# A spectral transform with a three-way maximum layer on one core: the input arrives as fp32, and GpSimd casts and turns it

## The chip, the cores and the metric

One core of a Trainium2 chip runs the kernel. The metric is the device time of one execution in microseconds. Three runs of the kernel before took 499.56, 500.29 and 500.31; their median, 500.29, is the time before.

## The reference

```python
x: (8, 3072, 256) fp32
X = np.fft.fft(np.fft.fft(x, axis=1), axis=2).real      # real part of the 2-D transform
x2 = X.reshape(24576, 256)
h = np.maximum(np.maximum(x2 @ w1, x2 @ w2), x2 @ w3)    # w1, w2, w3: 256 x 768
out = h @ w_out                                          # w_out: 768 x 256, fp32
```

So each batch of 3072 positions is transformed over its positions, then over its 256 channels, and the result goes through a feed-forward layer whose nonlinearity is a maximum of three products.

## The kernel before

**The transform over positions** has two stages, since 3072 is 24 times 128. A position is 128·a + bb. In the first stage (`fnet`, line 270) a matmul has as its stationary operand a 96 x 128 piece of the input: 96 partitions are 24 values of a for each of four groups g of 64 channels, and the 128 columns are the values of bb, for one of the 64 channels dl of each group. The moving operand is `m24blk`, a block-diagonal 96 x 96 table of the 24-point transform. So 64 matmuls make the first stage of a batch, one for each dl. They come in 13 groups (`DLS`, line 61), twelve of five matmuls and one of four, in an order that starts at the middle channels. Each group fills one of the two PSUM buffers of the pool `ps_f`, and ScalarE evicts it into `ub` as bf16 (line 272).

VectorE then folds channel d with channel 256 - d: sums go to `zE` and differences to `zO` (lines 280 to 297). That is possible because only the real part is wanted. The second stage multiplies zE and zO, as stationary operands with strided columns, with tables of cosines and sines (lines 318 to 326, 50 matmuls of mostly 128 columns, also through `ps_f`), which gives the tiles `tE` and `tO`, 128 x 1536 each, evicted by ScalarE (line 329). Three matmuls of one column (lines 332 to 334) make `t_mid`, the frequency at the middle. GpSimd copies tE and tO reversed to `tEr` and `tOr` (lines 339 and 340).

**The transform over channels** is not computed on the data: it is folded into the weights. `prep_first` (line 220) subtracts w1 from w2 and w3 on VectorE (line 228), multiplies the differences with the table `md` (line 232), and leaves `gE`, `gO` and `gD`. `prep_second` (line 240) makes `gw` and `gwr`, the product of md, w1 and w_out (lines 247 and 255). Both also take their PSUM from `ps_f`, and both run once, during batch 0.

**The layer.** Since max(a, b, c) = a + max(0, b - a, c - a), a block of 512 tokens needs for each of six columns blocks `jc` of the hidden layer only the two differences. A *unit* is one jc of one block; a batch has 18, three blocks of six. Its first half are four matmuls of 512 columns (lines 349 and 350) into two PSUM banks; ScalarE applies the relu to one of them (line 363), VectorE takes the maximum with the other into `hp` (line 364). Its second half are two more matmuls (line 357), which add gD to the same two banks and so turn the frequencies into their mirror images, and again a relu and a maximum, into `hm`. A batch has 108 unit matmuls. There are two pairs of these banks.

The output of a block is made of four pieces of 128 rows, twice 256 columns wide. Each half is eight matmuls of 256 columns (`l2_half`, lines 367, 369 and 372), so that a batch has 192 output matmuls. VectorE copies a piece out (line 392) and SP stores it (line 399) from one of four `ot` buffers, in two DMAs, or four for the last piece of a batch.

**What sets the order.** The units' loop pulls the output matmuls of earlier blocks from a list, eleven after each unit (`l2_some`, line 448), and the program is then ordered by the compiler's scheduler, which works from its own estimate of each instruction's length. Each engine runs its list in the order that comes out. On GpSimd the start of the program has an order fixed by hand (`manual_schedule`, line 133).

**The input.** `load_x0` (line 97) brings in a batch with 16 DMAs on GpSimd's software queue (line 105), which cast fp32 to bf16 on the way; rows of 64 channels stay together, so that a tile `x0` lies as (bb dl), and the stationary columns of the first stage, at `x0r[:, :, d0 + i]`, are 64 elements apart. There are two x0 buffers. Batches 0 and 1 are loaded at the start, with the weights between them on the same queue, and batch b + 2 after the first block of batch b.

Of the kernel before, what the change touches and what calls it, by code (L numbers as in the profile page):

```python
# [34 lines left out]
def kernel(  # L35
# [16 lines left out]
    nc = tc.nc  # L52

    B, S, D = x.shape
    assert (S, D) == (3072, 256)
    DFF = moe_w1.shape[1]
# [11 lines left out]
    ps_o = ctx.enter_context(tc.tile_pool(name="ps_o", bufs=2, space=bass.MemoryType.PSUM))  # L68
    x0_pool = ctx.enter_context(tc.tile_pool(name="x0", bufs=2))
# [14 lines left out]
    v2_bf = consts.tile([128, 2 * DFF], BF16, tag="v2_bf")  # L84
    v3_bf = consts.tile([128, 2 * DFF], BF16, tag="v3_bf")
# [11 lines left out]
    def load_x0(b, between):  # L97
        x0 = x0_pool.tile([96, 128 * 64], BF16, name="x0", tag="x0")
        xr = x[b].rearrange("(a bb) (g dl) -> g a bb dl", bb=128, g=4)
        x0v = x0.rearrange("p (bb dl) -> p bb dl", dl=64)  # L100
        for ch in range(4):
            if ch in between:
                between[ch]()
            for g in range(4):
                nc.gpsimd.dma_start(  # L105
                    out=x0v[g * 24:(g + 1) * 24, ch * 32:(ch + 1) * 32, :],
                    in_=xr[g, :, ch * 32:(ch + 1) * 32, :])
        return x0
# [17 lines left out]
    def between():  # L126

        nc.gpsimd.iota(kidx, [[1, 13], [24, 128]], base=0, channel_multiplier=0,
                       allow_small_or_imprecise_dtypes=True)
        nc.gpsimd.iota(dvec, [[1, 64], [64, 2]], base=0, channel_multiplier=0,  # L130
                       allow_small_or_imprecise_dtypes=True)

    with tc.manual_schedule(engines={mybir.EngineType.Pool}):
        x0_tiles = {0: load_x0(0, {1: between})}


        for jh in range(2):
            for wsrc, wdst in ((moe_w1, w1_bf), (moe_w2, w2_bf), (moe_w3, w3_bf)):
                nc.gpsimd.dma_start(
                    out=wdst.rearrange("p (fc j) -> p fc j", fc=2)[:, :, jh * 384:(jh + 1) * 384],  # L140
                    in_=wsrc.rearrange("(fc p) j -> p fc j", fc=2)[:, :, jh * 384:(jh + 1) * 384])
        nc.gpsimd.dma_start(out=wout_bf.rearrange("p (jc c) -> p jc c", jc=NJC),
                            in_=moe_w_out.rearrange("(jc p) c -> p jc c", jc=NJC))
        x0_tiles[1] = load_x0(1, {})
# [28 lines left out]
    for (dst, shift) in ((cos_t, 768.0), (sin_t, 0.0)):  # L173
        v = gen.tile([128, 13 * 128], FP32, name="v", tag="v", bufs=2)
        q = gen.tile([128, 13 * 128], FP32, name="q", tag="q", bufs=2)
# [14 lines left out]
    for fc in range(2):  # L190
# [10 lines left out]
        vi = gen.tile([128, 256], INT32, name="vi", tag="vi", bufs=2)  # L201
# [4 lines left out]
        _sin_of_index(nc, md[fc], vm, 256, neg_pi)  # L206

# [12 lines left out]
    def prep_first():  # L220

        for jh in range(2):
            cs = slice(jh * 384, (jh + 1) * 384)
            for i, (wv, vv) in enumerate(((w2_bf, v2_bf), (w3_bf, v3_bf))):
                w3d, v3d, w13d = (t.rearrange("p (fc j) -> p fc j", fc=2)[:, :, cs]
                                  for t in (wv, vv, w1_bf))
                tc.keep_in_program_order(
                    nc.vector.tensor_tensor(out=v3d, in0=w3d, in1=w13d, op=ALU.subtract))
# [8 lines left out]
                nc.vector.tensor_scalar(out=gD[i][:, cs], in0=gO[i][:, cs], scalar1=dif,  # L237
                                        scalar2=None, op0=ALU.mult)
# [25 lines left out]
    def fnet(b, x0):  # L264
        x0r = x0.rearrange("p (bb dl) -> p bb dl", dl=64)
        ub = u_pool.tile([128, 64 * 96], BF16, name="ub", tag="ub")
        for (d0, d1) in DLS:
            ps1 = ps_f.tile([128, 512], FP32, name="ps1", tag="ps")
            for i in range(d1 - d0):
                nc.tensor.matmul(ps1[:, i * 96:(i + 1) * 96], x0r[:, :, d0 + i], m24blk,  # L270
                                 start=True, stop=True)
            nc.scalar.copy(out=ub[:, d0 * 96:d1 * 96], in_=ps1[:, 0:(d1 - d0) * 96])  # L272
# [142 lines left out]

    l2_queue = []
# [9 lines left out]
    for b in range(B):  # L426
# [11 lines left out]
        for blk in range(3):  # L438
# [3 lines left out]
            for jc in range(NJC):  # L442
# [5 lines left out]
                l2_some(11)  # L448
            l2_some(1000)
# [5 lines left out]
            if blk == 0 and b + 2 < B:  # L455
                x0_tiles[b + 2] = load_x0(b + 2, {})
# [33 lines left out]
```

## Time and profile before

| What | us |
|---|---|
| the three runs | 499.56, 500.29, 500.31 |
| the profiled execution, its own time | 499.23 |
| its span | 497.1 |
| ScalarE's relu of a 512-column bank, mean | 0.588 |
| VectorE's maximum into hp, mean | 0.690 |
| GpSimd's DMA instructions, 128 of them, mean | 0.863 |
| GpSimd's reversed copies of tE, mean | 1.471 |

The mean granted clock of TensorE in that execution was 0.993.

How to read the views in the prediction: engines are PE (TensorE's matmuls), PEld (its weight loads), DVE (VectorE), ACT (ScalarE), POOL (GpSimd) and SP (which here only issues DMAs). A row of the time line has the start and the length in us, the engine, the line of the kernel, the operation, its output <- its inputs, the tile's shape and how many instructions the row joins; in brackets stands the idle time before it on that engine, and whose end released it. Matmuls are pipelined, and the ends of matmuls are modelled, so that rows overlap; the distance between two starts is the pace. A row of the windows has the window, its length, then busy time and instructions of PE, PEld, DVE, ACT, POOL and SP, then the granted clock, the busy share of the DMA engines and GB/s. A row of the groups has the count, then busy time and the mean in ns, then idle time ahead of the group and what ended it.

### The profile page before, as it was taken

Reading aid. Unit: us, or ns where it says so; the run is one execution under the profiler, and the core shown is the slowest. Engines: PE = TensorE matmul, PEld = TensorE weight load, DVE = VectorE, ACT = ScalarE, POOL = GpSimd, SP = SyncE. Lnnn points to the kernel's source line nnn. Section 1 sums busy time; section 2 is a strip of 40 time slices with the busy share of each in tenths; the row PEclk is TensorE's granted clock in tenths of the full one; section 3 lists DMA queues with packets and bytes.
Section 4 is the critical chain, followed back from the end, with each engine's and each line's share of the span. In section 5 each row is a group of like instructions: output and inputs, shape, how many; then the busy total and the mean of one; then the engine's idle time right before and its main releaser. Section 6 shows DMA issues by size and latency. Waiting matters only on the chain.

```text
span 497.1 us, 9195 instructions
## 1 busy us (share of the span) xinstructions
PE 453.5 (91%) x3408; PEld 315.6 (63%) x3408; DVE 320.4 (64%) x662; ACT 260.9 (52%) x472; POOL 140.6 (28%) x160
## 2 busy tenths in 40 slices
PE   0056999999999999999999999999999999999995
PEld 0055447785568657785669666875669566866664
DVE  8834674657676576657666567657675666667663
ACT  1355652575436653575446644665457644765440
POOL 9979800029000750029000840048000100020000
PEclk9999899999999999999999999999999999999998
DMA  8999992219921692219911793119911022102122
GB/s 48 75 164 99 98 32 86 84 44 108 105 86 66 59 133 99 73 44 109 126 65 65 74 123 102 65 46 120 134 64 65 22 65 84 65 22 65 65 84 86
DMA packets 163436, 40.05 MB, mean 81 GB/s; under 512 B 136512, under 2 KB 163392, under 8 KB 163392
## 3 DMA queue, kind: packets, MB, share of 16 engines
q0 software_dynamic: 135536, 14.30, 70.6%
q1 hardware_dynamic: 27856, 25.18, 16.1%
q8 instruction: 26, 0.43, 0.4%
q14 instruction: 18, 0.15, 0.1%
HBM read 28.31 MB, written 25.17 MB: 108 GB/s over the span
## 4 chain that ended last, share of the span: by engine, by line
PE 78%; DVE 3%; ACT 2%; POOL 2%; DMA 1%; issue 1%; DVEq 0%; ACTq 0%
PE po L372 23%; PE pse L349 12%; PE pse L357 11%; PE pse L350 11%; PE ps L270 8%; PE po L367 4%; PE po L369 4%; POOL x L105 2%; PE ps L318 2%; DMA x<-in_x_dram 1%; PE ps L324 1%; PE ps L326 1%; ACT stmp L363 1%; PE ps L321 1%; DVE zE L280 1%
## 5 line engine op out<-in xcount | busy, mean ns | idle before, releaser
L363 ACT ACTIVATE stmp<-pse 128x512 bf16<-128x512 f32 (+1 forms) x294 | 167.7, 588 | 164.3 <-PE pse L350 128.6
L364 DVE TENSOR_TENSOR hp<-pse,stmp 128x512 bf16<-128x512 f32 x144 | 99.1, 690 | 99.1 <-PE pse L357 39.8
L105 POOL DMA_DIRECT2D x<-in_x_dram x128 | 109.5, 863 | 8.1 <-DMA x<-in_x_dram 3.6
L349 PE MATMUL pse<-tE,gE 128*128 128x512 bf16 x288 | 108.8, 379 | 1.7 <-DVE hm L364 0.7
L350 PE MATMUL pse<-tO,gO 128*128 128x512 bf16 x288 | 109.1, 380 | 0.0
L364 DVE TENSOR_TENSOR hm<-pse,stmp 128x512 bf16<-128x512 f32 x144 | 99.0, 687 | 11.8 <-ACT stmp L363 9.3
L357 PE MATMUL pse<-tO,gD 128*128 128x512 bf16 x288 | 94.8, 380 | 1.1 <-ACT stmp L363 0.6
L339 POOL COPY tEr<-tE 128x1536 bf16<-128x1536 bf16 x8 | 11.8, 1471 | 289.1 <-ACT tE L329 289.1
L372 PE MATMUL po<-wout_bf,hp 128*128 128x256 bf16 x576 | 92.6, 272 | 0.0
L372 PE MATMUL po<-wout_bf,hm 128*128 128x256 bf16 x576 | 89.1, 272 | 0.1
L270 PE MATMUL ps<-m24blk,x 96*128 96x96 bf16 x512 | 57.4, 250 | 28.8 <-DMA w_bf<-in_moe_w_dram 27.5
L270 PEld LDWEIGHTS <-x 96*128 96x128 bf16 x512 | 55.9, 199 | 33.1 <-DMA w_bf<-in_moe_w_dram 27.4
L392 DVE COPY ot<-po 128x512 f32<-128x512 f32 x96 | 65.5, 684 | 14.5 <-PE po L372 13.8
L372 PEld LDWEIGHTS <-hm 128*128 128x128 bf16 x576 | 56.1, 99 | 17.3 <-DVE hm L364 0.4
L372 PEld LDWEIGHTS <-hp 128*128 128x128 bf16 x576 | 56.2, 100 | 14.2
L272 ACT CAST ub<-ps 128x480 bf16<-128x480 f32 (+1 forms) x104 | 55.4, 554 | 15.6 <-PE ps L270 13.3
L357 PEld LDWEIGHTS <-gD 128*128 128x128 bf16 x288 | 28.1, 98 | 29.8 <-issue 1.5
L350 PEld LDWEIGHTS <-gO 128*128 128x128 bf16 x300 | 29.4, 98 | 27.1 <-issue 12.2
L349 PEld LDWEIGHTS <-gE 128*128 128x128 bf16 x300 | 29.5, 99 | 21.1 <-issue 2.6
L280 DVE TENSOR_TENSOR zE<-ub 128x240 bf16<-128x240 bf16 (+2 forms) x80 | 20.2, 311 | 33.9 <-ACT ub L272 33.9
L367 PE MATMUL po<-gw,tE 128*128 128x256 bf16 x96 | 26.2, 272 | 0.0
L369 PE MATMUL po<-gwr,tOr 128*128 128x256 bf16 x96 | 26.2, 272 | 0.0
(99 smaller groups left out, 359.5 us busy)
## 6 DMA issues: line engine op xcount, KB each, us to landing
out_dram<-ot SPq DMA_DIRECT2D x176, 128.0 KB, 1.7
x<-in_x_dram POOLq DMA_DIRECT2D x128, 96.0 KB, 6.7
out_dram<-ot SPq DMA_DIRECT2D x24, 64.0 KB, 6.7
w_bf<-in_moe_w_dram POOLq DMA_DIRECT2D x6, 192.0 KB, 6.2
out_dram<-ot SPq DMA_DIRECT2D x8, 63.0 KB
wout_bf<-in_moe_w_out_dram POOLq DMA_DIRECT2D x1, 384.0 KB, 8.6
out_dram<-ot SPq DMA_DIRECT2D x1, 8.0 KB
```

Of the source, the lines that this page charges most:

```text
L105: nc.gpsimd.dma_start(out=x0v[g * 24:(g + 1) * 24, ch * 32:(ch + 1) * 32, :], in_=xr[g, :, ch * 32:(ch + 1) * 32, :])
L270: nc.tensor.matmul(ps1[:, i * 96:(i + 1) * 96], x0r[:, :, d0 + i], m24blk, start=True, stop=True)
L272: nc.scalar.copy(out=ub[:, d0 * 96:d1 * 96], in_=ps1[:, 0:(d1 - d0) * 96])
L349: nc.tensor.matmul(pse[:, 0:n], gE[i][:, js], te, start=True, stop=False)
L350: nc.tensor.matmul(pse[:, 0:n], gO[i][:, js], to, start=False, stop=True)
L357: nc.tensor.matmul(pse, gD[i][:, js], to, start=False, stop=True, skip_group_check=True)
L363: nc.scalar.activation(out=stmp[:, 0:n], in_=pses[0][:, 0:n], func=AX.Relu)
L364: nc.vector.tensor_tensor(out=dst, in0=src3, in1=stmp[:, 0:n], op=ALU.max)
L367: nc.tensor.matmul(po, te, gw[:, 0:256], start=True, stop=False)
L369: nc.tensor.matmul(po, to, wo, start=False, stop=False)
L372: nc.tensor.matmul(po, hcols(jc), wout_bf[:, jc * 256:(jc + 1) * 256], start=False, stop=(jc == NJC - 1))
L392: nc.vector.tensor_copy(out=ot, in_=po)
```

## The change

- The input comes as fp32, in four chunks of 32 values of bb for each batch (`load_chunk`), each four DMAs into one of four staging buffers `xs`. For batches 0 and 2 to 7 SP's hardware queue does it; batch 1's chunks are still issued on GpSimd.
- `turn_chunk` copies a chunk from xs to x0, casting it to bf16 and changing its layout from (bb dl) to (dl bb). GpSimd does it for all batches but the first; of batch 0 ScalarE takes half of chunks 1 and 2 and a third of chunk 3, VectorE another third of it.
- The first stage's stationary operand is now `x0r[:, d0 + i, :]`, 128 neighbouring elements.
- In batch b, after units 0 and 3 of blocks 0 and 1 (`TURNS`), one chunk of batch b + 2 is loaded on SP and turned on GpSimd.
- At the start the iotas stand ahead of the loads. Of GpSimd's list, three turns of batch 0 come first, then the weights, then the fourth turn, then batch 1's loads, each followed by its turn.
- `prep_first` subtracts in place and makes all four subtractions ahead of the matmuls; gD is made from PSUM instead of from gO. Two bf16 tiles (v2_bf, v3_bf) and second buffers of the tables' working tiles go.
- In batch 0 VectorE evicts five of the thirteen groups of the first stage.

```diff
+    xs_pool = ctx.enter_context(tc.tile_pool(name="xs", bufs=4))
...
-    def load_x0(b, between):
...
+    def load_chunk(b, ch, engine):
+        xs = xs_pool.tile([96, 32 * 64], FP32, name="xs", tag="xs")
+        xr = x[b].rearrange("(a bb) (g dl) -> g a bb dl", bb=128, g=4)
+        for g in range(4):
+            engine.dma_start(
+                out=xs[g * 24:(g + 1) * 24, :].rearrange("p (bb dl) -> p bb dl", dl=64),
+                in_=xr[g, :, ch * 32:(ch + 1) * 32, :])
+        return xs
+
+    def turn_chunk(xs, x0, ch, copies):
+        src = xs.rearrange("p (bb dl) -> p dl bb", dl=64)
+        dst = x0.rearrange("p (dl bb) -> p dl bb", bb=128)[:, :, ch * 32:(ch + 1) * 32]
+        step = 64 // len(copies)
+        for i, copy in enumerate(copies):
+            hi = 64 if i == len(copies) - 1 else (i + 1) * step
+            copy(dst[:, i * step:hi, :], src[:, i * step:hi, :])
...
+    x0_tiles = {0: new_x0(), 1: new_x0()}
+    first = [load_chunk(0, ch, nc.sync) for ch in range(4)]
...
+    with tc.manual_schedule(engines={mybir.EngineType.Pool}):
+        turn_chunk(first[0], x0_tiles[0], 0, [by_pool])
+        turn_chunk(first[1], x0_tiles[0], 1, [by_pool, by_act])
+        turn_chunk(first[2], x0_tiles[0], 2, [by_pool, by_act])
...
+        turn_chunk(first[3], x0_tiles[0], 3, [by_pool, by_dve, by_act])
+        for ch in range(4):
+            xs1 = load_chunk(1, ch, nc.gpsimd)
+            turn_chunk(xs1, x0_tiles[1], ch, [by_pool])
...
-        x0r = x0.rearrange("p (bb dl) -> p bb dl", dl=64)
+        x0r = x0.rearrange("p (dl bb) -> p dl bb", bb=128)
...
-                nc.tensor.matmul(ps1[:, i * 96:(i + 1) * 96], x0r[:, :, d0 + i], m24blk,
+                nc.tensor.matmul(ps1[:, i * 96:(i + 1) * 96], x0r[:, d0 + i, :], m24blk,
                                  start=True, stop=True)
-            nc.scalar.copy(out=ub[:, d0 * 96:d1 * 96], in_=ps1[:, 0:(d1 - d0) * 96])
+            copy = by_dve if b == 0 and d0 in (25, 35, 15, 10, 5) else by_act
+            copy(ub[:, d0 * 96:d1 * 96], ps1[:, 0:(d1 - d0) * 96])
...
+    TURNS = [(0, 0), (0, 3), (1, 0), (1, 3)]
...
+                if (blk, jc) in TURNS and b + 2 < B:
+                    ch = TURNS.index((blk, jc))
+                    if ch == 0:
+                        x0_tiles[b + 2] = new_x0()
+                    turn_chunk(load_chunk(b + 2, ch, nc.sync), x0_tiles[b + 2], ch, [by_pool])
...
-            if blk == 0 and b + 2 < B:
-                x0_tiles[b + 2] = load_x0(b + 2, {})
```

The scheduler orders the program anew. Three places matter for the prediction. Lines after the change are 24 to 27 higher in `fnet` and the layer: 296 is the first stage (270 before), 345 the second (318), 394 to 399 the output (367 to 372), 426 the store (399), 366 the reversed copy (339).

TensorE where batch 0 ends, in the kernel before: x0_149 is batch 1's input, and po_1160 an output piece of batch 0.

```order
L270 LDWEIGHTS x0_149
L270 MATMUL ps1_973<-m24blk_85,x0_149 128x96
L367 LDWEIGHTS tE_369
L367 MATMUL po_1160<-gw_104,tE_369 128x256
L369 LDWEIGHTS tO_370
L369 MATMUL po_1160<-gw_104,tO_370 128x256
L372 LDWEIGHTS hp_783
L372 MATMUL po_1160<-wout_bf_96,hp_783 128x256
...
L270 LDWEIGHTS x0_149
L270 MATMUL ps1_980<-m24blk_85,x0_149 128x96
```

There the output matmuls of batch 0 stand between the groups of batch 1's first stage. The same place after the change, where x0_125 is batch 1's input and po_1320 the last output piece of batch 0:

```order
L394 LDWEIGHTS tEr_458
L394 MATMUL po_1320<-gw_105,tEr_458 128x256
L396 LDWEIGHTS tOr_459
L396 MATMUL po_1320<-gwr_106,tOr_459 128x256
L399 LDWEIGHTS hm_812
L399 MATMUL po_1320<-wout_bf_97,hm_812 128x256
...
L296 LDWEIGHTS x0_125
L296 MATMUL ps1_987<-m24blk_88,x0_125 128x96
```

All 108 unit matmuls and all 192 output matmuls of batch 0 now stand ahead of batch 1's first stage.

GpSimd's list around batches 0 and 1 in the kernel before, where x0_149 and x0_596 are the inputs of batches 1 and 2:

```order
L105 DMA x0_149<-in_x_dram 24x32x64 x16
L339 COPY tEr_438<-tE_369 128x1536
L340 COPY tOr_439<-tO_370 128x1536
L105 DMA x0_596<-in_x_dram 24x32x64 x16
L339 COPY tEr_1145<-tE_1076 128x1536
```

After the change, the end of that stretch, where x0_125 is batch 1's input, x0_513 batch 2's, and xs_514 holds batch 2's first chunk:

```order
L116 CAST x0_125<-xs_251 96x64x32
L101 DMA xs_257<-in_x_dram 24x32x64 x4
L116 CAST x0_513<-xs_514 96x64x32
L116 CAST x0_125<-xs_257 96x64x32
L366 COPY tEr_1173<-tE_1104 128x1536
```

And SP's list after the change, where ot_1351 is the last piece of batch 0 and xs_562 batch 2's second chunk; in the kernel before this list holds stores alone:

```order
L426 DMA out_0_dram<-ot_1316 128x256 x2
L426 DMA out_0_dram<-ot_1351 64x256 x3
L426 DMA out_0_dram<-ot_1351 63x256
L101 DMA xs_514<-in_x_dram 24x32x64 x4
L101 DMA xs_562<-in_x_dram 24x32x64 x4
```

Batch 1's last turn stands behind batch 2's first one, and the load for that stands behind the stores of batch 0's last piece.

TensorE between the stages of batch 4 in the kernel before, where x0_2036 is batch 4's input and po_3355 and po_3390 are output pieces of batch 3:

```order
L270 MATMUL ps1_3202<-m24blk_85,x0_2036 128x96
L369 LDWEIGHTS tOr_2586
L369 MATMUL po_3355<-gwr_105,tOr_2586 128x256
L372 LDWEIGHTS hm_2944
L372 MATMUL po_3355<-wout_bf_96,hm_2944 128x256
...
L367 LDWEIGHTS tE_2516
L367 MATMUL po_3390<-gw_104,tE_2516 128x256
...
L372 MATMUL po_3390<-wout_bf_96,hp_2943 128x256
L318 LDWEIGHTS zE_3209
L318 MATMUL ps2_3238<-cos_t_88,zE_3209 128x128
```

After the change, where x0_1928 is batch 4's input:

```order
L296 LDWEIGHTS x0_1928
L296 MATMUL ps1_3248<-m24blk_88,x0_1928 128x96
...
L296 MATMUL ps1_3254<-m24blk_88,x0_1928 128x96
L345 LDWEIGHTS zE_3261
L345 MATMUL ps2_3290<-cos_t_91,zE_3261 128x128
```

The output matmuls that stood between the last groups and the second stage are gone from this place. In the whole list after the change, batch 2's first stage stands alone; those of batches 3 to 6 stand among four units, their last 25 matmuls and the second stage following one another without a break; batch 7's keeps output matmuls between its groups.

More of the change, by code (lines that the diff above doesn't have):

```diff
@@ L124 @@
     dvec = gen.tile([128, 128], FP32, tag="dvec")
[L126 to L144, printed above, removed]
+    nc.gpsimd.iota(kidx, [[1, 13], [24, 128]], base=0, channel_multiplier=0,
+                   allow_small_or_imprecise_dtypes=True)
+    nc.gpsimd.iota(dvec, [[1, 64], [64, 2]], base=0, channel_multiplier=0,
+                   allow_small_or_imprecise_dtypes=True)
+    x0_tiles = {0: new_x0(), 1: new_x0()}
+    first = [load_chunk(0, ch, nc.sync) for ch in range(4)]
     amod = gen.tile([96, 1], FP32, tag="amod")
@@ L236, in prep_first @@
                     nc.scalar.copy(out=dst[:, cs], in_=psg[:, 0:384])
-                nc.vector.tensor_scalar(out=gD[i][:, cs], in0=gO[i][:, cs], scalar1=dif,
-                                        scalar2=None, op0=ALU.mult)
+                    if half == 1:
+                        nc.vector.tensor_scalar(out=gD[i][:, cs], in0=psg[:, 0:384],
+                                                scalar1=dif, scalar2=None, op0=ALU.mult)
     def prep_second():
```

48 lines of the change are left out of this document (27 added, 21 removed).

## The prediction

> **What bounds the kernel now.** I read the page's span, engines and chain first, then the windows, then the time line at the places that the change touches.
>
> ```profile
> span 497.1 us, 9195 instructions
> PE 453.5 (91%) x3408; PEld 315.6 (63%) x3408; DVE 320.4 (64%) x662; ACT 260.9 (52%) x472; POOL 140.6 (28%) x160
> PE 78%; DVE 3%; ACT 2%; POOL 2%; DMA 1%; issue 1%; DVEq 0%; ACTq 0%
> ```
>
> ```profile
> 132.00:187.00 55.00, 54.63 (x419) 38.44 (x417) 35.78 (x73) 30.43 (x56) 15.76 (x18) 1.00 0.77 87
> ```
>
> From the second batch on TensorE is the bound: 78% of the chain is its work, and in a stretch of one batch it is busy 54.63 of 55 us. That figure flatters it, since the end of a matmul is modelled and short gaps vanish. So I price its work by the distance between starts.
>
> ```profile
> 68.13 0.38 PE L357 MATMUL pse<-tO,gD 128*128 128x512 bf16 x1
> 68.35 0.38 PE L349 MATMUL pse<-tE,gE 128*128 128x512 bf16 x1
> 68.56 0.38 PE L350 MATMUL pse<-tO,gO 128*128 128x512 bf16 x1
> ...
> 77.33 0.38 PE L367 MATMUL po<-gw,tEr 128*128 128x256 bf16 x2
> ...
> 82.60 0.27 PE L367 MATMUL po<-gw,tEr 128*128 128x256 bf16 x1
> ...
> 83.47 0.27 PE L367 MATMUL po<-gw,tE 128*128 128x256 bf16 x1
> ...
> 430.22 0.57 PE L270 MATMUL ps<-m24blk,x 96*128 96x96 bf16 x5
> 430.62 0.28 PE L372 MATMUL po<-wout_bf,hm 128*128 128x256 bf16 x1
> 430.82 1.08 ACT L272 CAST ub<-ps 128x480 bf16<-128x480 f32 x2 [0.17 <-PE ps L270]
> ```
>
> A unit matmul (lines 349, 350, 357; 512 columns) costs 0.216 us. An output matmul (lines 367 to 372; 256 columns) costs 0.109 us: eight between 82.60 and 83.47. A first-stage matmul with its strided stationary costs 0.080 us, five in 0.40, while ScalarE needs 0.54 us to evict such a group.
>
> The first rows tell one thing more. From 68.13 to 77.33 stand 30 unit matmuls, five units' worth, with no output matmul between them. They are 6.5 us of work and take 9.2: 1.84 us a unit instead of 1.30, because a unit waits for ScalarE, VectorE and its PSUM banks. **A unit without output matmuls beside it loses 0.55 us.** The output matmuls are the filler of this kernel.
>
> ```profile
> 105.04 0.28 PE L318 MATMUL ps<-cos_t,zE 128*128 128x128 bf16 x1
> 436.18 0.28 PE L318 MATMUL ps<-cos_t,zE 128*128 128x128 bf16 x1
> ...
> 440.58 0.21 PE L334 MATMUL ps<-cos_t,zO 128*128 128x1 bf16 x1
> ```
>
> Six batches pass between the first two rows, 55.2 us each. A batch has 108 unit matmuls (23.3 us), 192 output matmuls (20.9), 64 of the first stage (5.1) and a second stage of 3.7 (4.4 us from 436.18 to the end at 440.6, less three other matmuls and the last ones): 53.0. The other 2.2 us are four units without filler. So the prices close.
>
> **The order is the change that counts.** TensorE runs its instructions in the order printed above. In the kernel before, the first stage of a batch is laced with output matmuls of the batch ahead. After the change batch 1's stands behind all of batch 0's output, batch 2's stands alone, and those of batches 3 to 6 stand among four units, their last 25 matmuls and the second stage back to back. What a transform costs with nothing between its parts, batch 0 shows.
>
> ```profile
> 27.46 1.09 PE L270 MATMUL ps<-m24blk,x 96*128 96x96 bf16 x10 [27.46 <-DMA w_bf<-in_moe_w_dram]
> 28.76 1.06 PE L270 MATMUL ps<-m24blk,x 96*128 96x96 bf16 x10 [0.21 <-ACT ub L272]
> ...
> 35.68 0.56 ACT L272 CAST ub<-ps 128x480 bf16<-128x480 f32 x1 [0.31 <-PE ps L270]
> ...
> 37.30 0.33 PE L318 MATMUL ps<-cos_t,zE 128*128 128x128 bf16 x1 [1.66 <-DVE zE L292]
> ...
> 42.59 0.20 PE L334 MATMUL ps<-cos_t,zO 128*128 128x1 bf16 x1
> ```
>
> It takes 15.2 us, 27.5 to 42.7: 8.2 until the last group, 1.7 for the fold, 5.3 for the second stage at a slow pace. Laced, the same is 8.8 (5.1 and 3.7). Two groups take 1.25 us through two PSUM buffers, and the eviction is half of it.
>
> *Contiguous stationaries.* The nearest rows with one are eight columns wide:
>
> ```profile
> 480.39 0.17 PE L349 MATMUL pse<-t_mid,gE 128*128 128x8 bf16 x1
> 480.42 0.17 PE L350 MATMUL pse<-t_mid,gO 128*128 128x8 bf16 x1
> ```
>
> They start 0.03 us apart, so such a load costs at most that. Ninety-six columns stream in 0.040 (96/256 of an output matmul). The pitch is then between 0.040, the load hidden, and 0.080, no gain; I take 0.045, as the load hides fully behind 256 columns. That is 2.2 us a batch where TensorE is the limit. It is so only in batch 7. In a row by itself the stage is held by the eviction: 13 groups at 0.55, 7.2 us instead of 8.2. The Trainium skill speaks against the gain: "TensorE: Matmul & The Clock Gate" (Weight-path perf modes) says that the fast weight load is on for 128 columns that are not fp32, "packed or strided". By that rule the pitch stays at 0.080 and the sum is about 4 us higher. The rows 0.03 and 0.080 apart side with the change, though no row has the same width.
>
> *The start.* First stage at 27.5 now.
>
> ```profile
> 3.04 3.50 DVE L23 TENSOR_SCALAR mask<-vm 96x24 f32<-96x24 f32 x1
> ...
> 7.24 15.68 POOL L105 DMA_DIRECT2D x<-in_x_dram  x12
> ...
> 22.55 0.51 ACT L30 ACTIVATE md<-vm,neg_pi 128x256 bf16<-128x256 f32 x1 [1.15 <-DVE vm L205]
> ```
>
> The issue of 16 loads on GpSimd goes, and with it VectorE's stall of 3.3 us. But the tables now stand ahead of the last turning pieces on VectorE and ScalarE, so the start can't come before their end, 23.1 less 3.3, plus about 1.5: 21.3. GpSimd's turning of 4,096 elements (3.9 us at the rate below, 8 at half of it) may hold VectorE as its DMA issue did: up to 29. I take 24.5. Batch 0's transform keeps its 15.2 (splitting evictions with VectorE doesn't shorten a buffer's round), to 39.7.
>
> *Weights' preparation and batch 0.*
>
> ```profile
> 43.20:53.50 10.30, 6.71 (x24) 2.60 (x24) 6.31 (x8) 4.39 (x11) 10.25 (x13) 0.83 2.69 94
> ```
>
> TensorE is idle 3.6 us here. The subtractions stand together now and GpSimd issues less beside them, so I let 2 of these go (0 to 3.6). Work until batch 0's last output matmul: 23.3 + 20.9 + 5.2 for 40 preparing matmuls (16 of 384 columns at 0.163, by columns, and 24 of 256 at 0.109), and 4 us of stalls with the first block's units: 53.5, to 93.2.
>
> *The new wait.* Batch 1's fourth piece is turned on GpSimd behind batch 2's first, whose load stands on SP behind batch 0's last four stores. The chain is: copy of the last output, four stores, four loads, landing, two turns, first stage.
>
> ```profile
> L392 DVE COPY ot<-po 128x512 f32<-128x512 f32 x96 | 65.5, 684 | 14.5 <-PE po L372 13.8
> L339 POOL COPY tEr<-tE 128x1536 bf16<-128x1536 bf16 x8 | 11.8, 1471 | 289.1 <-ACT tE L329 289.1
> ```
>
> ```profile
> 437.76 0.81 SPq L399 DMA_DIRECT2D out_dram<-ot  x2
> ```
>
> ```profile
> DMA to landing us min/median/max: 3.2/6.7/9.4
> ```
>
> Copy 0.7, eight issues at 0.4, landing 3.2 to 9.4, two turns. A turn of 2,048 elements is 2.0 us at GpSimd's 0.96 ns an element, 4 at twice that, for the fp32 and the stride of 256 bytes have no row. Sum 11 to 21; I take 5 for the landing and 3 a turn: **15 us**, with TensorE having nothing else in its queue. The Trainium skill's "GPSIMD Engine Reference" (Performance pitfalls) gives about 2.9 cycles an element for strides over 8 bytes, an estimate of 4.9 us a turn; the wait would be 19. To 108.2.
>
> *The transforms without filler.* Batch 1: 15.3, to 123.5. Then 108 unit and 96 output matmuls (33.8), four bare units (2.2), batch 2's transform at 7.2 + 1.7 + 4.5 (between 3.7 and 5.3): 13.4, to 172.9. Up to the end of batch 3's: 57 unit and 128 output matmuls (26.3), six bare units (3.3), and a section of 17: among four units ScalarE has eight groups at 0.54 and eight activations at 0.59 (below), 9 us against 7 of TensorE; five groups alone 2.8; fold 1.7; second stage 3.7. To 219.5.
>
> ```profile
> L363 ACT ACTIVATE stmp<-pse 128x512 bf16<-128x512 f32 (+1 forms) x294 | 167.7, 588 | 164.3 <-PE pse L350 128.6
> ```
>
> Batches 4, 5 and 6 repeat with 85 unit and 192 output matmuls (39.3), twelve bare units (6.6) and 17: 62.9 each, 8 more than now, to 408.2. The last step has 136 unit and 328 output matmuls (65.2), twelve bare units, a laced transform (64 x 0.045 + 3.7) and 1.3 for the rest: 79.7, to 487.9. The tail after 440.8 stays: 56.3. Span **544**, and 2.1 around it (499.23 for the profiled run): **546 us**, against the profiled run, which is 1.1 below the median of the three.
>
> **Rivals.**
> *The gain wins.* Seven batches at 2.2 us, 3 at the start, 2 in the preparation: 478. It needs the wait at batch 1 and the bare units to sum to under 20 us. For it: the pitch rows. Against it: the printed order leaves TensorE nothing to do in that wait, whose floor is 11 us, and the bare run at 68 us is measured. Chance 0.06.
> *Bare units run at VectorE's pace,* two passes of 0.69, 1.38 a unit: 58 such units lose 0.09 instead of 0.55, 27 us less, 519. Against it: the bare stretch quoted ran at 1.84. Chance 0.13.
> *Slow turns and a blocked SP queue.* Turns of 5 us and loads of 768 short rows that issue slower than stores of 128: the wait grows by 4, and in the long runs of output matmuls, where a store is due every 0.9 us, a load waiting ahead of it holds the four output buffers for about 3 us a batch: 562. It decides if a load blocks SP over 7 us, four outputs at 1.75. Chance 0.12.
> *The weight load was fast already* (the rule on packed or strided patterns: the pitch stays 0.080): batch 7 gains nothing, batch 2's transform and the dense ends little, 550. Chance 0.07.
>
> **How the numbers follow.** Forecast 546, chance 0.62. Its open terms are the start (-3, +5), the wait (-4, +6), the section of 17 (2 each, four times) and the bare units' loss (a sixth of 32). Down to the second rival it reaches 517, up to the third 568; outside lie the first and the far ends. A measurement here tells about 0.2%. Faster 0.06, same 0.01, slower 0.93.
>
> **What would show it.** TensorE's first L296 of batch 1 waits about 15 us for GpSimd near 93 us, and GpSimd for a load; first-stage rows without L394 to L399 between them, ten in about 1.1 us; starts 0.045 apart within a group; turns of 2 to 4 us; the distance between second stages 60 to 65 us for batches 4 to 6. It is wrong if that wait is under 8 us, or if those distances stay near 55.

## The result, and the profile after

The changed kernel takes 560.82 us (median of four runs, 558.66 to 562.66) against 499.93 before: 1.122 times as long, 95% interval 1.117 to 1.127. The forecast was 546, with a range of 517 to 568. The profiled execution took 558.66, with a span of 556.8.

The page of the kernel after, in the lines that answer to those of before:

```profile
span 556.8 us, 9215 instructions
PE 467.6 (84%) x3408; PEld 308.7 (55%) x3408; DVE 324.9 (58%) x668; ACT 259.3 (47%) x470; POOL 157.6 (28%) x80
PE 67%; ACT 14%; DVE 7%; SPq 3%; issue 3%; DMA 2%; POOL 2%; ACTq 0%; DVEq 0%; POOLq 0%
```

TensorE's share of the chain falls from 78% to 67%, and ScalarE's rises from 2% to 14%: work that lay beside TensorE's now lies on the path. The windows of the stages show where (length of the window; busy time of PE, PEld, DVE, ACT and POOL; granted clock; DMA). The ends of the windows are the ends of batch 0's transform, of its output, the start of batch 1's first stage, and the ends of the transforms of batches 1, 2, 4, 5, 7.

```profile
45.20:96.70 51.50, 50.86 (x343) 33.18 (x342) 33.38 (x52) 26.94 (x50) 22.21 (x16) 1.00 0.53 99
96.70:115.70 19.00, 0.06 (x2) 0.04 (x2) 0.69 (x1) 0.00 (x0) 7.16 (x2) 0.56 0.85 128
115.70:130.70 15.00, 12.09 (x118) 10.50 (x119) 5.26 (x26) 9.53 (x18) 1.47 (x1) 0.53 0.91 130
130.70:182.30 51.60, 46.82 (x325) 29.12 (x324) 32.42 (x68) 30.68 (x56) 13.96 (x5) 0.90 0.44 79
293.50:356.90 63.40, 58.12 (x421) 37.27 (x420) 36.51 (x74) 30.17 (x56) 17.13 (x7) 0.97 0.49 100
500.30:556.80 56.50, 50.67 (x358) 32.98 (x356) 34.00 (x57) 22.67 (x44) 1.47 (x2) 0.97 0.21 66
```

The second row is the new wait: 19.0 us in which TensorE does nothing. Batch 5 takes 63.4 us (fifth row) where a batch took 55.2 before; the tail is as long as it was. The chain of waits in the gap (start, length, what):

```profile
96.76 0.70 DVE ot L419
97.48 0.53 SPq L426
...
99.33 0.50 SPq L426
...
100.07 0.34 SPq L101
...
101.01 0.89 SPq L101
101.95 6.34 DMA xs<-in_x_dram
...
112.00 3.62 POOL x L116
115.66 0.59 PE ps L296 x5
```

That is the chain of the forecast, link by link: the copy of the last output, four stores, four loads, the landing, two turns, the first stage. The first turn is the 3.44 us of "issue" ahead of 112.00, as GpSimd's time line shows:

```profile
108.44 7.16 POOL L116 CAST x<-xs 96x2048 bf16<-96x2048 f32 x2 [27.05 <-DMA xs<-in_x_dram]
```

The time line of TensorE in batch 4 shows the rest: the last groups of the first stage wait for ScalarE, the second stage waits for the fold, and its matmuls start 0.11 us apart.

```profile
284.70 0.83 PE L296 MATMUL ps<-m24blk,x 96*128 96x96 bf16 x10 [0.24 <-ACT ub L122]
285.72 0.83 PE L296 MATMUL ps<-m24blk,x 96*128 96x96 bf16 x9 [0.19 <-ACT ub L122]
288.21 0.33 PE L345 MATMUL ps<-cos_t,zE 128*128 128x128 bf16 x1 [1.66 <-DVE zE L319]
288.34 0.31 PE L348 MATMUL ps<-sin_t,zE 128*128 128x128 bf16 x1
```

### The profile page after: what moved, and what is told of

It is laid out like the page before. It is cut to its first block, busy times and chain, and to the rows that moved or that the text cites. A ratio compares the mean times of both kernels' runs of the same rounds, so it can differ in the third digit from the quotient of the medians.

```text
span 556.8 us, 9215 instructions
## 1 busy us (share of the span) xinstructions
PE 467.6 (84%) x3408; PEld 308.7 (55%) x3408; DVE 324.9 (58%) x668; ACT 259.3 (47%) x470; POOL 157.6 (28%) x80
## 4 chain that ended last, share of the span: by engine, by line
PE 67%; ACT 14%; DVE 7%; SPq 3%; issue 3%; DMA 2%; POOL 2%; ACTq 0%; DVEq 0%; POOLq 0%
PE po L399 22%; PE pse L376 10%; ACT stmp L390 9%; PE pse L377 9%; PE pse L384 8%; ACT ub L122 5%; PE po L394 4%; DVE hp L391 4%; PE po L396 4%; PE ps L296 3%; SPq L101 3%; DMA xs<-in_x_dram 2%; PE ps L345 2%; DVE hm L391 2%; PE ps L351 2%
## 5 line engine op out<-in xcount | busy, mean ns | idle before, releaser
L116 POOL CAST x<-xs 96x2048 bf16<-96x2048 f32 (+2 forms) x32 | 114.0, 3587 | 50.1 <-DMA xs<-in_x_dram 50.1
L377 PE MATMUL pse<-tO,gO 128*128 128x512 bf16 x288 | 107.7, 378 | 0.0
L384 PE MATMUL pse<-tO,gD 128*128 128x512 bf16 x288 | 98.3, 378 | 5.9 <-ACT stmp L390 2.8
L296 PE MATMUL ps<-m24blk,x 96*128 96x96 bf16 x512 | 43.3, 226 | 56.4 <-POOL x L116 48.3
L399 PE MATMUL po<-wout_bf,hp 128*128 128x256 bf16 x576 | 83.9, 272 | 0.0
L399 PE MATMUL po<-wout_bf,hm 128*128 128x256 bf16 x576 | 83.3, 273 | 0.0
L296 PEld LDWEIGHTS <-x 96*128 96x128 bf16 x512 | 34.6, 109 | 72.7 <-POOL x L116 48.6
L122 ACT CAST ub<-ps 128x480 bf16<-128x480 f32 (+1 forms) x99 | 51.6, 555 | 34.8 <-PE ps L296 33.6
L384 PEld LDWEIGHTS <-gD 128*128 128x128 bf16 x288 | 27.8, 97 | 36.0 <-issue 7.8
L345 PE MATMUL ps<-cos_t,zE 128*128 128x128 bf16 (+1 forms) x104 | 20.1, 284 | 11.9 <-DVE zE L319 11.6
L394 PE MATMUL po<-gw,tEr 128*128 128x256 bf16 x96 | 26.2, 273 | 0.0
```

The source lines that it names most:

```text
L116: nc.gpsimd.tensor_copy(out, in_)
L122: nc.scalar.copy(out=out, in_=in_)
L296: nc.tensor.matmul(ps1[:, i * 96:(i + 1) * 96], x0r[:, d0 + i, :], m24blk, start=True, stop=True)
L345: nc.tensor.matmul(outsl, er[:, :, r], cos_t[:, k0:k0 + w], start=True, stop=not two)
L377: nc.tensor.matmul(pse[:, 0:n], gO[i][:, js], to, start=False, stop=True)
L384: nc.tensor.matmul(pse, gD[i][:, js], to, start=False, stop=True, skip_group_check=True)
```

## The experiments

Every kernel was timed beside the kernel before, which took 499.2 to 500.2 us in these sessions. "Bare units" are counted from the compiled order: unit matmuls with no output matmul between them, beyond the first six of a stretch, in units of six.

**1. The contiguous stationary alone.** The kernel before reads neighbouring elements; nothing is turned.

```diff
-        x0r = x0.rearrange("p (bb dl) -> p bb dl", dl=64)
+        x0r = x0.rearrange("p (dl bb) -> p dl bb", bb=128)
-                nc.tensor.matmul(ps1[:, i * 96:(i + 1) * 96], x0r[:, :, d0 + i], m24blk,
+                nc.tensor.matmul(ps1[:, i * 96:(i + 1) * 96], x0r[:, d0 + i, :], m24blk,
```

> The kernel before, whose first stage takes 128 neighbouring elements of x0 as stationary columns; x0 is not turned, so the transform works on the wrong elements, with the same number and shapes of instructions. Theory (a contiguous stationary saves 0.038 us a matmul wherever the first stage stands among output matmuls): 64 x 0.038 = 2.4 us a batch, 17 for seven batches, less about 4 because the order has 8 more bare units: 484 to 492. Rival (the weight load is equally fast for strided columns, and nothing is gained): 500 to 504. Starts within a group 0.042 us apart by the theory, 0.080 by the rival.

Measured: 486.43 us, ratio 0.974 (0.970 to 0.978). The weight loads of the first stage, by line (count; shortest, median and longest in ns), in the kernel before and in this one:

```profile
L270 PEld LDWEIGHTS <-x x512: 161/209/239, 27.4 to 434.2; 96*128 96x128 bf16 x171
```

```profile
L270 PEld LDWEIGHTS <-x x512: 94/97/146, 19.7 to 422.1; 96*128 96x128 bf16 x171
```

The load takes less than half. The rival is out. But not all of the 13 us are its doing: the elements that the first two groups read here all lie in the second of the four chunks, so that the first stage starts at 19.7 instead of 27.5, and batch 0's transform ends 4.6 us earlier. From the end of batch 1's transform to that of batch 7's it takes 322.3 us against 331.2: 1.5 us a batch, with 8 more bare units in the order.

**2. Cast without turning.** The changed kernel, whose copies keep the old layout, with the old strided columns; TensorE's order is the same row by row.

```diff
-        src = xs.rearrange("p (bb dl) -> p dl bb", dl=64)
-        dst = x0.rearrange("p (dl bb) -> p dl bb", bb=128)[:, :, ch * 32:(ch + 1) * 32]
+        src = xs.rearrange("p (bb dl) -> p bb dl", dl=64)
+        dst = x0.rearrange("p (bb dl) -> p bb dl", dl=64)[:, ch * 32:(ch + 1) * 32, :]
...
-                nc.tensor.matmul(ps1[:, i * 96:(i + 1) * 96], x0r[:, d0 + i, :], m24blk,
+                nc.tensor.matmul(ps1[:, i * 96:(i + 1) * 96], x0r[:, :, d0 + i], m24blk,
```

> The changed kernel whose copies cast to bf16 but keep the layout (bb dl), so that the first stage has its old strided stationary columns; TensorE's order of kinds is unchanged. Theory (TensorE's order and the wait at batch 1 set the time, the turning itself hardly does): each copy falls from 3.6 to between 2.0 and 2.7 us and the wait at batch 1 by 2 to 3, and the strided columns give about 1 us back in each of seven batches: 558 to 566, the same as the changed kernel within 1%. Rival (the turning with its large stride on GpSimd is what costs, by its own time and by holding VectorE): 20 us or more faster, under 541.

Measured: 562.82 us, ratio 1.127 (1.122 to 1.132). GpSimd's copies in the changed kernel, then here:

```profile
L116 POOL CAST x<-xs x32: 1329/3712/5069, 9.1 to 432.4; 96x2048 bf16<-96x2048 f32 x29, 96x1024 bf16<-96x1024 f32 x2, 96x672 bf16<-96x672 f32 x1
```

```profile
L116 POOL CAST x<-xs x32: 1033/1890/3304, 9.1 to 428.9; 96x2048 bf16<-96x2048 f32 x29, 96x1024 bf16<-96x1024 f32 x2, 96x640 bf16<-96x640 f32 x1
```

The turning doubles a copy, from 1.89 to 3.71 us. Halving it shortens the wait at batch 1 (15.2 us here, 3.8 less, where 2 to 3 were expected) and the strided columns take that back later, about 1 us a batch. So neither the turns' length nor the layout explains the 61 us; what both kernels share does. Nor do the turns cost by holding VectorE's folds: in the trace of the changed kernel no fold lies beside a turn.

**3 and 4. The loads on another queue.** Batches 2 to 7 are loaded on ScalarE's queue; in the second kernel batch 1's loads are also issued together.

```diff
-                    turn_chunk(load_chunk(b + 2, ch, nc.sync), x0_tiles[b + 2], ch, [by_pool])
+                    turn_chunk(load_chunk(b + 2, ch, nc.scalar), x0_tiles[b + 2], ch, [by_pool])
```

> The changed kernel whose loads of batches 2 to 7 are issued on ScalarE's queue instead of SP's; nothing else is edited, and the compiler's order then has 14 bare units instead of 72 and output matmuls between the first stage's groups from batch 2 on. Theory (loads behind stores on SP made the order, and the order costs the time): batch 1's wait falls from 19 to about 9 since its load needn't wait for stores, the batches after it take about 53 us: 496 to 512. Rival (fp32 loads and turning on GpSimd limit the kernel whatever the order): over 545. Against the theory by its own side effect: 16 issues of up to 0.8 us a batch on ScalarE, up to 12 us a batch, delay evictions; then 520 to 540.

> As the run with ScalarE's queue, and batch 1's four chunks are also issued one after the other ahead of their four turns. Theory: the wait at batch 1 and the cold clock behind it go (batch 1's first stage then stands among outputs of batch 0): 10 to 20 us under the run with ScalarE's queue alone, 482 to 495, so faster than the kernel before. Rival (the wait at batch 1 is only moved: batch 2's data then come late): the same as that run within 4 us.

Measured: 551.8, 552.8 and 553.2 us and once 542.8 for the first, too wide apart for an interval; 542.2 us for the second (538.7 to 546.9), ratio 1.083 (1.077 to 1.090). What issuing batch 1's loads together is worth stays open: the fastest runs of the two are 4 us apart. **Both expectations of the theory failed**: the order lost its bare stretches (14 and 19 bare units), and most of the time stayed. The second kernel's profile has three reasons beside the start. What TensorE waited for (us in total, times, longest):

```profile
PE ps L296 <- POOL x L116: 30.5, 1, 30.5
PE pse L376 <- ACT stmp L390: 15.3, 1, 15.3
```

The first row is the start. The second is ScalarE: ahead of a relu stand sixteen issues of loads, the last twelve of which follow one another from 89.06 to 105.55, up to 2.0 us each, and TensorE waits 15.3 us for that relu in batch 1. Then, in a batch of 59.2 us, VectorE and GpSimd:

```profile
325.18 3.70 POOL L116 CAST x<-xs 96x2048 bf16<-96x2048 f32 x1 [9.80 <-DMA xs<-in_x_dram]
...
353.33 3.71 POOL L116 CAST x<-xs 96x2048 bf16<-96x2048 f32 x1 [14.54 <-PE ps L296]
```

```profile
326.45 0.69 DVE L391 TENSOR_TENSOR hp<-pse,stmp 128x512 bf16<-128x512 f32 x1 [0.75 <-PE pse L377]
...
350.50 0.86 DVE L307 TENSOR_TENSOR zE<-ub 128x240 bf16<-128x240 bf16 x4 [1.41 <-ACT ub L122]
...
354.15 3.62 DVE L307 TENSOR_TENSOR zO<-ub 128x240 bf16<-128x240 bf16 x4
```

Four folding operations take 0.86 us, and 3.62 when they start beside a turn: the first of them takes 3.04 and ends 0.15 us after the turn, and the others follow. A maximum, which reads PSUM, takes its 0.69 us beside a turn all the same. The Trainium skill ("SBUF — State Buffer", SBUF: two separate sides) says that VectorE and GpSimd have one pair of ports in common, which one instruction holds to its end while the other engine's waits, and that VectorE needs it only in some of its modes or with two inputs in SBUF; these rows agree. The third reason is the order itself: it gives a unit two output matmuls at a time, and such units run at 2.04 us (maxima into hp start at 324.41, 326.45 and 328.49). So a queue that takes the loads off SP is no clean test if it delays something else.

**5. The weights' preparation alone,** in the kernel before; the order is the same otherwise.

```diff
+        for cs in halves:
+            for vv in diffs:
...
+                    nc.vector.tensor_tensor(out=v3d, in0=v3d, in1=w13d, op=ALU.subtract))
...
-                nc.vector.tensor_scalar(out=gD[i][:, cs], in0=gO[i][:, cs], scalar1=dif,
+                    if half == 1:
+                        nc.vector.tensor_scalar(out=gD[i][:, cs], in0=psg[:, 0:384],
```

> The kernel before with only the weights' preparation of the change (four subtractions first, in place, gD from PSUM); the order of the rest is unchanged. Theory (it lets go of 2 of the 3.6 us in which TensorE stands idle there): 496.5 to 499, against 499.2 for the kernel before. Rival (another wait ends there, GpSimd's DMA issue or the loads of the weights): no change, within 1 us. Nothing here can explain the 61 us either way.

Measured: 493.67 us, ratio 0.988 (0.985 to 0.991): 6 us, three times the expectation. In the kernel before, VectorE's first gD reads gO from SBUF and is held while GpSimd works (its two reversed copies end at 47.82, the gD at 47.94); TensorE waits for the subtraction behind it and then runs at half clock (window, busy times, granted clock 0.54):

```profile
44.73 3.21 DVE L237 TENSOR_SCALAR gD<-gO,dif 128x384 bf16<-128x384 bf16 x1 [6.00 <-ACT gO L236]
```

```profile
48.46 0.81 PE L232 MATMUL psg<-v_bf,md 128*128 128x384 bf16 x4 [3.05 <-DVE v_bf L228]
```

```profile
50.00:53.50 3.50, 3.32 (x9) 1.22 (x8) 2.51 (x6) 1.46 (x3) 3.50 (x6) 0.54 1.69 97
```

**6. The wait at batch 1 alone.** In the changed kernel the four loads of batch 1 go ahead of its four turns on GpSimd; later loads stay on SP.

```diff
-        for ch in range(4):
-            xs1 = load_chunk(1, ch, nc.gpsimd)
-            turn_chunk(xs1, x0_tiles[1], ch, [by_pool])
+        xs1 = [load_chunk(1, ch, nc.gpsimd) for ch in range(4)]
+        for ch in range(4):
+            turn_chunk(xs1[ch], x0_tiles[1], ch, [by_pool])
```

> The changed kernel whose four loads of batch 1 are issued ahead of its four turns on GpSimd; loads of later batches stay on SP. Theory (the wait of 19 us at batch 1 is paid once and isn't hidden elsewhere): batch 1's first stage then stands among outputs of batch 0, batches 2 and later run as before at 63 us, and 14 to 22 us of the time go: 538 to 547. Rival (the wait only moves to batch 2, whose loads stand on SP behind the same stores): 556 or more.

Measured: 546.06 us in one run. TensorE waits for GpSimd only at the start:

```profile
PE ps L296 <- POOL x L116: 29.6, 1, 29.6
```

The wait at batch 1 is gone, about 15 us with it, and batches 4 to 6 take 63 to 64 us as before: the wait and the slow batches are two things. The 15 us are a net figure, since the order changes as well: it has 89 bare units instead of 72, batch 1's transform stands among output matmuls, and batch 3 takes 63.6 us instead of 47.4.

**7. The loads on GpSimd's queue,** with its order of 36 bare units instead of 72 and with output matmuls between the groups.

```diff
-                    turn_chunk(load_chunk(b + 2, ch, nc.sync), x0_tiles[b + 2], ch, [by_pool])
+                    turn_chunk(load_chunk(b + 2, ch, nc.gpsimd), x0_tiles[b + 2], ch, [by_pool])
```

> The changed kernel whose fp32 loads of batches 2 to 7 are issued on GpSimd's queue instead of SP's; turns stay on GpSimd. TensorE's order then has the first stage dense among 24 output matmuls, 14 more ahead of the second stage, and 36 bare units instead of 72. Theory (the order costs the time): batches of about 54 instead of 63.5 us, the wait at batch 1 stays at 10 to 20: 500 to 522. Rival, from the runs with ScalarE's queue (fp32 staging and turning cost it themselves: the turns hold VectorE's folding for 3 us each time they meet, and loads come late): batches of 58 us or more, 530 or over.

Measured: 516.52 us in one run, 44 less than the changed kernel with the same loads, turns and layout. The total came as the theory had it, the parts did not: batch 1's wait vanished (its last turn no longer stands behind a load that waits for stores), and the batches take 56 to 61 us instead of 54. Two batches that follow one another, and what makes the longer one:

```profile
229.97:290.06 60.09, 55.67 (x420) 36.53 (x419) 39.56 (x74) 30.41 (x57) 36.02 (x27) 0.97 0.62 116
290.06:346.13 56.07, 54.63 (x421) 35.61 (x419) 36.28 (x74) 30.42 (x57) 30.61 (x22) 1.00 0.57 114
```

The same 74 operations on VectorE take 39.56 us in one and 36.28 in the other. Batch 2 is one of the longer ones, and shows why: one folding operation of 24 columns, 0.16 us long elsewhere, starts while GpSimd turns.

```profile
163.76 3.73 POOL L116 CAST x<-xs 96x2048 bf16<-96x2048 f32 x1 [5.28 <-DMA xs<-in_x_dram]
```

```profile
163.94 3.58 DVE L316 TENSOR_TENSOR zE<-ub 128x24 bf16<-128x24 bf16 x1
```

**8. The old preparation in the changed kernel.**

```diff
-                        nc.vector.tensor_scalar(out=gD[i][:, cs], in0=psg[:, 0:384],
-                                                scalar1=dif, scalar2=None, op0=ALU.mult)
+                nc.vector.tensor_scalar(out=gD[i][:, cs], in0=gO[i][:, cs], scalar1=dif,
+                                        scalar2=None, op0=ALU.mult)
```

> The changed kernel with the old order of the weights' preparation (subtractions between the matmuls, gD from gO); TensorE's kinds stand in the same order. Theory (the new preparation is worth 6 us beside GpSimd's loads and is a gain in the changed kernel as well): 564 to 568 against 560.8. Rival (in the changed kernel GpSimd issues fewer loads there, and VectorE isn't held): 559 to 562.

Measured: 565.82 us, ratio 1.134 (1.130 to 1.137), so 5.0 more than the changed kernel. Its first gD and, for comparison, that of the changed kernel, which reads PSUM, both beside a turn on GpSimd:

```profile
47.95 3.75 DVE L259 TENSOR_SCALAR gD<-gO,dif 128x384 bf16<-128x384 bf16 x1 [5.55 <-ACT gO L258]
```

```profile
47.21 0.62 DVE L263 TENSOR_SCALAR gD<-psg,dif 128x384 bf16<-128x384 f32 x1 [4.39 <-ACT gO L261]
47.21 3.71 POOL L116 CAST x<-xs 96x2048 bf16<-96x2048 f32 x1
```

**9, 10, 12. Turning elsewhere.** The kernel before with its casting loads into bf16 staging tiles, the new preparation, the tables' working tiles without second buffers, batch 0 used unturned, and batches 1 to 7 turned one batch ahead: in four pieces on ScalarE, in 16 pieces on VectorE, and in 16 pieces on the two in turn. In the first:

```diff
+                if (blk, jc) in TURNS and b + 1 < B:
...
+                    turn_chunk(raw_tiles[b + 1], x0_tiles[b + 1], ch, [by_act])
```

In the other two:

```diff
+                            turn_piece(raw_tiles[b + 1], x0_tiles[b + 1], p, 16, by_dve)
```

```diff
+                            turn_piece(raw_tiles[b + 1], x0_tiles[b + 1], p, 16, by_dve if p % 2 else by_act)
```

> The kernel before with its casting loads on GpSimd's queue, into bf16 staging tiles; ScalarE turns batches 1 to 7 into the contiguous layout one batch ahead, in four pieces; batch 0 is used unturned with strided columns; the weights' preparation as in the change. The order keeps output matmuls between the groups of the first stage, with 19 bare units against 16. Theory (the contiguous layout is worth 2.4 us a batch where the order is kept, and a turn off TensorE's path costs nothing): 480 to 490. Rival (four turns of about 2 us a batch on ScalarE delay evictions and relus, and give it back): 496 or more.

> As the run that turns on ScalarE, but VectorE turns batches 1 to 7, in 16 pieces of 512 elements a batch instead of four of 2,048; the order has 15 bare units and output matmuls between the first stage's groups. Theory (a turn hurts by how long it holds the engine that a unit waits for; pieces of 0.6 us hide): the weights' preparation is worth 6, the contiguous layout 2.2 in each of seven batches: 476 to 485. Rival (VectorE's copies of bf16 wait for GpSimd's loads as its other bf16 work does, and the maxima behind them wait too): 490 or more.

> As the run with 16 small turns a batch on VectorE, but every other piece goes to ScalarE. Theory (what the small turns cost is the time by which they hold up the maxima on VectorE, so that halving VectorE's share gives about half of the 2 us a batch back): 486 to 491, under the run with all pieces on VectorE. Rival (each piece of about 0.9 us on ScalarE holds a relu as long as a piece on VectorE holds a maximum, and nothing is gained): 492 to 498.

Measured: 533.07 us (ratio 1.065, 1.061 to 1.069), 493.91 (0.988, 0.986 to 0.990) and 503.63 (1.008, 1.005 to 1.011). All three missed the theory's numbers. The pieces, in the order of the three kernels (ScalarE, VectorE, and ScalarE's in the third):

```profile
L124 ACT COPY x<-xr x28: 3663/3724/3877, 46.8 to 431.3; 96x2048 bf16<-96x2048 bf16 x28
```

```profile
L120 DVE COPY x<-xr x112: 565/596/789, 48.0 to 403.8; 96x512 bf16<-96x512 bf16 x112
```

```profile
L123 ACT COPY x<-xr x56: 1030/1076/1137, 46.9 to 397.7; 96x512 bf16<-96x512 bf16 x56
```

A turn keeps ScalarE from its relus for 3.7 us, and TensorE's wait for relus in the first of the three kernels adds up to 31 us (22.4 ahead of line 382 and 8.7 ahead of line 374). On VectorE the cost is spread thin, but it takes back all that the layout gives, and more: the kernel is as fast as the preparation alone (493.67), although its first stage starts 2.3 us earlier (25.5 against 27.8). Moving half of the pieces to ScalarE made it slower: a piece there is longer by four fifths, up to four of them stand in a row, and TensorE's wait for relus comes to 13 us.

**11. Dense transforms without bare stretches.** As run 9, with the turns on GpSimd in four pieces. The order has 16 bare units, like the kernel before, and nothing between the groups of batches 1 to 6.

```diff
-                    turn_chunk(raw_tiles[b + 1], x0_tiles[b + 1], ch, [by_act])
+                    turn_chunk(raw_tiles[b + 1], x0_tiles[b + 1], ch, [by_pool])
```

> The same loads and staging, but GpSimd turns, in four pieces a batch; the order then has all first stages of batches 1 to 6 behind all outputs of the batch ahead, with nothing between their groups, and 16 bare units as in the kernel before. It takes the dense transform apart from the bare units. Theory (a transform without filler costs 13.4 to 15 us instead of 6.4 laced): batches 1 to 6 about 60 us each, the last laced: 512 to 530. Rival (only bare units cost, a dense transform doesn't): 480 to 495.

Measured: 516.03 us in one run, as the theory had it; batches 2 to 6 take 59.7 us on average, and no fold lies beside a turn. What TensorE waits for there, beyond the start:

```profile
PE ps L343 <- DVE zE L317: 11.7, 7, 1.7
PE ps L295 <- ACT ub L297: 8.3, 36, 0.4
```

## Why the prediction was right

**The order.** Right, and run 7 is the strongest evidence: the queue of the loads changes the order and the place of the issue, nothing else, and 44 us go. No run changes the order and leaves the issue where it is, and runs 3 and 4 show that the place of the issue can cost as much by itself. Run 11 takes the slow batches apart: a transform without filler costs about 4 us a batch (59.7 against 55.2, although its columns are contiguous), and the bare stretches of the changed kernel the other 4 (63.4). That split is a difference between kernels, not a price: in the changed kernel four units stand among the groups and hide part of the transform.

From the end of batch 3's transform to batch 4's first stage 39.3 us of matmuls at the forecast's prices take 46.3 (229.74 to 276.04). The 7.0 more answer to the forecast's 6.6 for twelve units in two runs without output matmuls: 0.58 each, against 0.55 forecast. The rival that had them at VectorE's pace is out. One step of the working isn't borne out: the 2.2 us a batch that its prices leave over in the kernel before were put down to four units without filler, but that order has 16 bare units in all, ten of them in batch 0. The sum doesn't rest on it, as the loss was read from the stretch at 68 us.

**The wait at batch 1.** Forecast 15, measured 19.0, with every link present. Three terms were too small: eight issues and their gaps took 4.5 us instead of 3.2, the landing 6.3 instead of 5, a turn 3.6 instead of 3. The rule of the Trainium skill on strides ("GPSIMD Engine Reference", Performance pitfalls) gave, as estimates, 4.9 us a turn and 19 us in all; the total agrees by chance, the turn doesn't (3.71). Run 6, without the wait, is about 15 us faster in spite of 17 more bare units.

**The rival of slow turns and a blocked SP queue.** Its 562 lies nearer to the measured 560.8 than the forecast does, but not by its mechanism. The wait did grow by its 4 us, though not through turns of 5 us. Its other half, output buffers held by loads ahead of stores, didn't happen: the whole list of TensorE's waits in the changed kernel has none for VectorE's copy of an output piece, and VectorE's copies wait for TensorE alone.

**The pitch.** 0.045 forecast. In batch 7, where output matmuls stand between the groups, five matmuls take 0.21 us, 0.042 each (0.080 in batch 1, where the granted clock is 0.50):

```profile
489.78 0.37 PE L296 MATMUL ps<-m24blk,x 96*128 96x96 bf16 x5
489.99 0.27 PE L394 MATMUL po<-gw,tEr 128*128 128x256 bf16 x1
```

The rival took from the Trainium skill ("TensorE: Matmul & The Clock Gate", Weight-path perf modes: "packed or strided") that strided columns load as fast. With a step of 64 elements they don't: run 1 has the loads at 97 ns against 209. That rival is out.

**The sections.** All stages but the start and the wait came within 2.3 us of their forecast: batch 1's transform 15.1 (15.3), the stretch to the end of batch 2's 51.6 (49.4), to batch 3's 47.4 (46.6), batches 4 to 6 at 63.4 to 63.8 (62.9), the last step 80.0 (79.7). One cause inside a section was not foreseen: in the second stage the clock falls.

```profile
285.70:288.20 2.50, 0.70 (x9) 0.44 (x8) 2.10 (x13) 1.42 (x3) 0.00 (x0) 0.72 0.70 92
288.20:290.70 2.50, 2.49 (x24) 2.47 (x25) 2.17 (x10) 1.10 (x2) 0.00 (x0) 0.50 0.01 3
```

TensorE is busy for 0.70 of 2.5 us before it, and the granted clock is 0.50 in the next window. The forecast had the second stage at 3.7 us in these sections; it takes 5.3 in batch 4. That the section still came out near (17.5 us, against 17) is luck: its other terms were 1.1 us too large together.

**What was mis-sized.** The span came out 12.8 us above the forecast 544. The start is the largest part, 29.4 instead of 24.5:

```profile
24.12 5.01 ACT L122 CAST x<-xs 96x1024 bf16<-96x1024 f32 x3
26.84 0.80 DVE L119 CAST x<-xs 96x672 bf16<-96x672 f32 x1 [2.67 <-DMA xs<-in_x_dram]
27.16 0.87 POOL L223 DMA_DIRECT2D wout_bf<-in_moe_w_out_dram  x1
28.00 1.33 POOL L116 CAST x<-xs 96x672 bf16<-96x672 f32 x1
```

The forecast built its start on the end of the tables and had no term for the loads of batch 0. SP needs until 21.4 to issue the sixteen of them, up to 1.6 us each, and VectorE gets the fourth chunk at 26.84. Then two turning pieces end together: ScalarE's third one at 29.13, since its three stand behind the tables and take 5.0 us where the forecast had about 1.5, and GpSimd's at 29.33, behind the issue of seven loads of weights. Moving GpSimd's piece out of that queue alone would therefore give about 0.2 us. Then the wait (+4.0), batches 2 to 6 (+4.9 together), and in the other direction batch 0 (-2.0): the preparation was worth 5 to 6 us instead of 2 (runs 5 and 8). By the rows the larger part is that gD no longer reads SBUF, which the forecast priced only as a change of order; no run tries that operand apart from the order of the subtractions.

**What stays open.** Where within VectorE's list run 10 loses what the contiguous columns give is not shown: TensorE's waits for maxima are small, none over 0.7 us and 5.8 us in all, and nothing was tried on them by itself. What is said of runs 6, 7 and 11 rests on one execution each.

## What to carry to other kernels

A change of a load's queue can reorder every engine: on SP, ScalarE and GpSimd the same loads of batches 2 to 7 gave 72, 14 and 36 bare units. So compare the order of the bound engine before and after such a change. Count what stands without filler, since work that fills the gaps between short dependent steps has a price when it goes (here about half a microsecond a unit). The best version found is the smallest part of this change, the weights' preparation alone (493.67 us, ratio 0.988), most of it, by its rows, from where one operand is read.

## What the runs showed of the hardware

- A copy of 96 x 2048 fp32 to bf16 on GpSimd takes 1.89 us in order and 3.71 with a step of 64 elements on the read side; ScalarE needs 3.72 for as many bf16 elements with that step, VectorE 0.60 and ScalarE 1.08 for 512.
- In these traces a bf16 fold or gD of VectorE on SBUF that starts while a GpSimd copy is under way ends when the copy does (a fold of 0.16 us became 3.58, four of 0.86 became 3.62); one that reads its first operand from PSUM isn't held (0.62 and 0.69 us beside a copy).
- A weight load of 96 partitions and 128 columns takes 97 ns with neighbouring elements and 209 ns with a step of 64.
- SP needs 0.43 us (median) to issue a store of the output and 1.05 us, at most 3.0, to issue an fp32 load of a quarter of a chunk.
